# Two FFN layers behind a decayed linear attention: the first two token blocks of layer 1 run in two parts each, with partial sums in SBUF

## The chip, the cores and the metric

The kernel runs on one core of a Trainium2 chip. The metric is the device time of one execution in microseconds (us). Three runs of the kernel before took 987.18, 989.37 and 989.90 us; the median is 989.37 us. A core has the engines PE (matrix multiply, with a separate weight load, PEld), DVE (vector), ACT (scalar), POOL and SP. DMAs are issued from the instruction stream of an engine; here SP issues nearly all of them.

## The reference

```
x = attention(q, k, v, alpha)     # (4, 8, 768, 48); state = alpha_t * state + k_t v_t^T ; y_t = q_t state
x = x.transpose(0, 2, 1, 3).reshape(3072, 384)
h = x @ w_in ; x = max(0.01 * h, h) @ w_out              # layer 1: 384 -> 2048 -> 384
h = x @ moe2_w_in ; x = elu(h) @ moe2_w_out              # layer 2: the same sizes
```

All data are float32, except that the weights come to the chip as pairs of 32-bit words (a float64 each) and are turned there into a high and a low float32r part. Every FFN product is three matmuls: high times high, low times high, high times low.

## The kernel before, in words

**Attention.** The 3072 tokens are 24 units of 128 tokens (`NU`), six to a batch row; a unit holds all 8 heads, as four pairs on partitions 0 to 47 and 64 to 111. `attn_prep` (lines 124 to 138) makes two running products of the decay on DVE (two scans of 1.2 us) and scales k and q. `attn_S` computes the scores of the four pairs and a transpose of k on PE; `attn_S_post` masks them on DVE and, when there is a state from the unit before, makes the decayed state T (lines 166 to 170) in two instructions, one per head of the pair, into a block-diagonal tile with zeros elsewhere. `attn_V` multiplies by v, adds the part of the state (line 186, over all 112 partitions of T) and forms the new state's addend `pu` (line 193). `attn_V_post` writes the result as a high and a low part into the x tiles `xh` and `xl`, and makes the new state S in two instructions (lines 207 to 212).

**Blocks of layer 1.** Four units are one block of 512 tokens; there are six. A unit writes its 384 rows as 3 times 112 partitions and a rest; `gather` (lines 215 to 218) moves the rest into place by six DMAs for `xh` and six for `xl`, on SP's queue. `x` has two buffers, so the units of block j+2 can write only when block j has been read for the last time. A block has 16 steps (m = 0 to 15, a slice of 128 of the 2048 hidden features). Step (j, m) is `ffn1_h` (nine matmuls), `ffn1_g` (an ACT and a DVE instruction, then the split into high and low on ACT and DVE), and `ffn1_y` (nine matmuls into three PSUM banks, which are copied to `x2t` at m = 15, line 288). The h part runs two steps ahead of the y part (`LA`).

**Weights of layer 1.** Slice m of both matrices arrives raw, 768 KB in five DMAs from SP (`stage1`, lines 413 to 421), in one of four tiles `x2t[0..3]`, which later take the results of layer 1. `convert_p` (ACT, lines 232 and 233), `convert_a` (DVE lines 237, 238 and 240, ACT line 241) and `convert_b` (DVE line 244) turn it into the two parts in SBUF; `x2t[4]` and `x2t[5]` are its scratch. When slice m is done, slice m + 4 is loaded. `conv_to` is called in the head (up to 4 slices by the fourth unit) and then ahead of each step of block 0, up to slice s + 5, so that all 16 slices are converted in the steps of block 0.

**Order.** `seq` (lines 615 and 616) is the order of steps: block 0 with all m, block 1 with all m, and so on, then layer 2. The 20 units after the first four are cut in four pieces each (`pieces`), and those of block j + 1 are spread over block j (lines 633 to 637). The order written is a program order: the Tile framework gives every instruction a place on its engine by its own simulated timeline, and may place work of another kind earlier when what it needs is there. Only instructions passed to `pin` keep their program order.

**Loads.** `next_load(u + 3)` after unit u issues the load of `pack` (674 KB) and of `v` (288 KB) on SP. Three buffers each.

**Guard.** In layer 2 the kernel reads all decay data again (`guard_load`, 24 `span` tiles from the pool of `pack`, three buffers) and checks it with two ACT instructions each (`guard_unit`); a slow path `general()` runs only where the check fails. Lines 668 to 676 place one unit every second step from block 1 of layer 2 on. The pool of `pack` also holds half of the output tiles `osb` at each block's end (line 349).

Of the kernel before, what the change touches and what calls it, by code (L numbers as in the profile page):

```python
# [19 lines left out]
def attention_two_layers_kernel(  # L20
# [42 lines left out]
    causal = const.tile([128, C], F32, name="causal")  # L63
    T = const.tile([PR, NP, PD], F32, name="T")
    d0 = const.tile([PR, EXT], F32, name="d0")
# [19 lines left out]
    def constants():  # L85
        make_identity(nc, ident)
        nc.gpsimd.memset(causal, 1.0)
        nc.gpsimd.affine_select(
            out=causal, in_=causal, compare_op=ALU.is_ge, fill=0.0,
            base=0, pattern=[[1, C]], channel_multiplier=-1,  # L90
        )
        nc.gpsimd.memset(T, 0.0)
# [11 lines left out]

    def load_unit(u, first=False):
        t = pack_p.tile([PR, EXT + 2 * NP * C], F32, tag="pack", name="pack")
        if first:
            m = EXT + NP * C
            nc.sync.dma_start(t[:, 0:EXT], seqs[u, :, 0:EXT])
            nc.scalar.dma_start(t[:, EXT:m], seqs[u, :, EXT:m])  # L110
            nc.sync.dma_start(t[:, m:], seqs[u, :, m:])
        else:
            nc.sync.dma_start(t, seqs[u])
        packs[u] = t

    def load_v(u):
        t = v_p.tile([128, NP, 3 * D], F32, tag="v", name="vt")
        nc.sync.dma_start(t.rearrange("s p e -> s (p e)"), vals[u])
        vts[u] = t
# [37 lines left out]
    def attn_S_post(u):  # L157
# [8 lines left out]
        if c > 0:  # L166
            for j in range(2):
                r = slice(64 * j, 64 * j + D)
                nc.vector.tensor_mul(
                    T[r, :, j * D:(j + 1) * D], st["S"][r], d["pe"][r].to_broadcast([D, NP, D]))  # L170

    def attn_V(u):
# [10 lines left out]
        if c > 0:  # L183
            for p in range(NP):
                for j in range(2):
                    nc.tensor.matmul(po[64 * j:64 * j + D, p], lhsT=T[:, p, j * D:(j + 1) * D], rhs=qh[:, p],  # L186
                                     start=False, stop=(p == NP - 1), skip_group_check=True)
        d["po"] = po
        if c < NC - 1:
            pu = ps_a.tile([PR, NP, D], F32, tag="at", name="pu")  # L190
            for p in range(NP):
                for j in range(2):
                    nc.tensor.matmul(pu[64 * j:64 * j + D, p], lhsT=d["kn"][:, p, 64 * j:64 * j + D],
                                     rhs=vt[:, p, 2 * j * D:(2 * j + 1) * D], start=(p == 0), stop=(p == NP - 1),
# [3 lines left out]
    def attn_V_post(u, xh, xl, off):  # L198
# [5 lines left out]
        if c < NC - 1:  # L204
            pu = d["pu"]
            Sn = at_p.tile([PR, NP, D], F32, tag="S", name="S")
            for j in range(2):
                r = slice(64 * j, 64 * j + D)
                if c > 0:
                    nc.vector.tensor_add(Sn[r], pu[r], T[r, :, j * D:(j + 1) * D])  # L210
                else:
                    nc.vector.tensor_copy(Sn[r], pu[r])
# [39 lines left out]
    def ffn1_h(j, m):  # L252
        xh, xl, n = xt[j]
        hp = ps_h.tile([128, n], F32, tag="h", name="hp")
# [19 lines left out]
    ytiles = {}  # L274

    def ffn1_y(j, m):
        n = xt[j][2]
        gh, gl = steps.pop((1, j, m))
        if m == 0:
            ytiles[j] = [ps_y.tile([128, n], F32, tag=f"y{c}", name=f"y{c}") for c in range(KD)]  # L280
        wh, wl = wout[m]
        for c in range(KD):
            for i, (a, x) in enumerate(((wh, gh), (wl, gh), (wh, gl))):
                nc.tensor.matmul(  # L284
                    ytiles[j][c], lhsT=a[:, c * 128:(c + 1) * 128], rhs=x,
                    start=(m == 0 and i == 0), stop=(m == KF - 1 and i == 2),
                )
        if m == KF - 1:
# [8 lines left out]
    def x2_split(j):  # L297
        xh = xs_p.tile([128, KD, 512], F32R, tag="xh", name="xh")
        xl = xs_p.tile([128, KD, 512], F32R, tag="xl", name="xl")
        for c in range(KD):  # L300
# [70 lines left out]
    def xtile(j):  # L371
        if j not in xt:
            n = blocks[j][1] * C
            xt[j] = (
                xs_p.tile([128, KD + 1, 512], F32R, tag="xh", name="xh"),
                xs_p.tile([128, KD + 1, 512], F32R, tag="xl", name="xl"),
                n,
            )
        return xt[j]
# [7 lines left out]
    def attn_post(u, i):  # L387
# [5 lines left out]
        elif i == 2:  # L393
            j = unit_block[u]
            xh, xl, _ = xtile(j)
            attn_V_post(u, xh, xl, (u - blocks[j][0]) * C)
            if u == blocks[j][0] + blocks[j][1] - 1:
                for x in (xh, xl):
                    gather(x, blocks[j][1] * C)
# [57 lines left out]
    class Conversions:  # L457
# [46 lines left out]
    def general():  # L504
# [52 lines left out]
        for j in range(NB):  # L557
            xt.pop(j)
            xh, xl, n = xtile(j)
            for i in range(n // C):  # L560
# [20 lines left out]
    with ExitStack():  # L581
# [25 lines left out]
        for u in range(4):  # L607
# [21 lines left out]
        for s, e in enumerate(seq):  # L629
# [3 lines left out]
            if ph == 1 and pieces:  # L633
                tgt = blocks[j + 1][1] * 4
                done = tgt - len([p for p in pieces if unit_block[p[0]] <= j + 1])
                want = min(tgt, -(-tgt * (m + 1) // (KF - LA)))
# [9 lines left out]
            for p in now:  # L646
                attn_post(*p)
# [18 lines left out]
            if ph == 2 and m == 4 and (j + 1) * 512 < NT:  # L666
                x2_split(j + 1)
            if ph == 2 and j > 0:
                u, odd = divmod(after - 2 * KF, 2)
                if u <= NU and not odd:  # L670
                    if u < NU:
                        guard_load(u)
                    if u > 0:
                        guard_unit(u - 1)
                if u == NU + 1 and not odd:
                    guard()
# [86 lines left out]
```

## Time and profile before

| | us |
|---|---|
| median of three runs | 989.37 |
| the profiled execution | 987.68 |
| its span, first to last instruction | 986.0 |
| PE busy in it | 934.5 (95%) |
| DVE busy | 545.6 (55%) |
| ACT busy | 446.6 (45%) |
| first FFN matmul begins | 59.83 |
| results of block 0 copied out of PSUM from | 190.04 |

The span is the time between the first and the last instruction of the profiled execution; 1.7 us lie around it. Shares of busy time are means over all stages. A matmul's record holds its latency, so that the sum of PE's busy time counts a queue of matmuls as one stretch, and the mean of one record is longer than the distance between two.

### The profile page before, as it was taken

The numbers are of one execution on the slowest core, as the hardware profiler recorded it, in microseconds if no ns is written. First come the engines' busy times: TensorE is split into PE (matmuls) and PEld (weight loads), VectorE is DVE, ScalarE is ACT, GpSimd is POOL, SyncE is SP. The second block draws the span as 40 slices with busy tenths as digits, with TensorE's granted clock in tenths as the row PEclk, the third lists the DMA queues.
The fourth block names the chain that finished last, engine by engine and source line by source line (L and its number), as shares of the span: only waits on it lengthen the run. The fifth ranks groups of instructions, "written<-read, shape, count | busy, mean of one in ns | idle before, by whom it ended". The sixth has DMA issues, their size and how long they took to land.

```text
span 986.0 us, 13236 instructions
## 1 busy us (share of the span) xinstructions
PE 934.5 (95%) x5234; PEld 790.4 (80%) x5234; DVE 545.6 (55%) x916; ACT 446.6 (45%) x783; POOL 1.4 (0%) x9
## 2 busy tenths in 40 slices
PE   4689979899999999999999999999999999999996
PEld 3567757688788788888878889989989989899996
DVE  6799998533657556555559993433433333433332
ACT  1245453332322322233458874574574674444442
POOL 0000000000000000000000000000000000000000
PEclk9779998899999999999999999999999999999999
DMA  9655571000211212211134310030110210000001
GB/s 238 161 173 163 149 184 61 13 1 19 68 51 42 57 41 81 55 44 49 49 96 145 112 49 1 4 105 1 53 55 1 78 30 1 33 1 1 32 1 37
DMA packets 25671, 62.40 MB, mean 63 GB/s; under 512 B 4512, under 2 KB 7584, under 8 KB 25600
## 3 DMA queue, kind: packets, MB, share of 16 engines
q1 hardware_dynamic: 25472, 61.24, 22.0%
q8 instruction: 43, 0.70, 0.3%
q10 hardware_dynamic: 128, 0.23, 0.1%
q14 instruction: 28, 0.23, 0.1%
HBM read 54.37 MB, written 4.72 MB: 60 GB/s over the span
## 4 chain that ended last, share of the span: by engine, by line
PE 80%; DMA 9%; DVE 6%; ACT 2%; SPq 1%; issue 1%; DVEq 0%; ACTq 0%
PE y L284 19%; PE hp L259 18%; PE hp L313 18%; PE o L344 9%; PE oa L344 9%; DMA pack<-in_seqs_dram 3%; DMA x2t<-in_w_dram 3%; PE sc L149 2%; PE po L181 2%; DMA span<-in_seqs_dram 2%; PE po L186 1%; DMA out_dram<-osb 1%; ACT span L496 1%; DVE A L161 1%; DVE x2t L240 1%
## 5 line engine op out<-in xcount | busy, mean ns | idle before, releaser
L82 DVE TENSOR_TENSOR gl<-t,gh 128x512 fp32r<-128x512 f32 x192 | 132.1, 690 | 130.5 <-ACT gh L79 118.9
L79 ACT CAST gh<-t 128x512 fp32r<-128x512 f32 x192 | 118.9, 620 | 170.9 <-PE y L284 60.9
L284 PE MATMUL y<-gh,w 128*128 128x512 f32 x576 | 172.9, 398 | 2.9 <-ACT gh L79 2.9
L259 PE MATMUL hp<-xh,w 128*128 128x512 f32 x576 | 155.1, 402 | 4.6 <-DVE t L268 2.4
L313 PE MATMUL hp<-xh,w 128*128 128x512 f32 x576 | 149.2, 394 | 1.2 <-DVE t L322 1.2
L322 DVE SCALAR_TENSOR_TENSOR t<-t,hp 128x512 f32<-128x512 f32 x96 | 66.0, 687 | 152.2 <-ACT t L321 152.2
L259 PEld LDWEIGHTS hp<-xh,w 128*128 128x128 f32 x576 | 108.8, 192 | 29.6 <-issue 3.2
L284 PEld LDWEIGHTS y<-gh,w 128*128 128x128 f32 x576 | 107.2, 190 | 26.9 <-ACT gh L79 3.7
L313 PEld LDWEIGHTS hp<-xh,w 128*128 128x128 f32 x576 | 106.5, 188 | 19.0 <-DVE t L322 2.2
L284 PE MATMUL y<-gl,w 128*128 128x512 f32 x288 | 105.2, 399 | 0.4 <-DVE gl L82 0.4
L320 ACT ACTIVATE t<-hp 128x512 f32<-128x512 f32 x96 | 57.0, 594 | 105.8 <-PE hp L313 105.7
L268 DVE TENSOR_TENSOR t<-t,hp 128x512 f32<-128x512 f32 x96 | 65.2, 681 | 59.3 <-ACT t L267 59.1
L344 PE MATMUL oa<-w,gh 128*128 128x384 f32 x384 | 96.3, 337 | 1.3 <-ACT gh L79 1.3
L267 ACT ACTIVATE t<-hp 128x512 f32<-128x512 f32 x96 | 56.4, 596 | 90.7 <-PE hp L259 90.5
L344 PE MATMUL o<-w,gh 128*128 128x384 f32 x384 | 95.1, 337 | 1.9 <-ACT gh L79 1.9
L259 PE MATMUL hp<-xl,w 128*128 128x512 f32 x288 | 83.4, 393 | 0.0
L313 PE MATMUL hp<-xl,w 128*128 128x512 f32 x288 | 81.9, 392 | 0.0
L344 PEld LDWEIGHTS o<-w,gh 128*128 128x128 f32 x384 | 70.5, 188 | 7.7 <-ACT gh L79 2.7
L344 PEld LDWEIGHTS oa<-w,gh 128*128 128x128 f32 x384 | 70.1, 188 | 4.5 <-ACT gh L79 1.7
L284 PEld LDWEIGHTS y<-gl,w 128*128 128x128 f32 x288 | 53.6, 189 | 13.6 <-DVE gl L82 1.3
L313 PEld LDWEIGHTS hp<-xl,w 128*128 128x128 f32 x288 | 54.1, 188 | 12.2
L259 PEld LDWEIGHTS hp<-xl,w 128*128 128x128 f32 x288 | 54.3, 189 | 11.7 <-issue 0.2
(94 smaller groups left out, 1005.6 us busy)
## 6 DMA issues: line engine op xcount, KB each, us to landing
pack<-in_seqs_dram SPq DMA_DIRECT2D x23, 674.2 KB, 5.6
stg<-in_w_dram SPq DMA_DIRECT2D x28, 384.0 KB, 3.1
x2t<-in_w_dram SPq DMA_DIRECT2D x20, 384.0 KB, 4.6
vt<-in_vals_dram SPq DMA_DIRECT2D x24, 288.0 KB, 5.1
span<-in_seqs_dram SPq DMA_DIRECT2D x24, 226.2 KB, 2.7
x2t<-in_w_dram SPq DMA_DIRECT2D x32, 144.0 KB, 4.5
out_dram<-osb SPq DMA_DIRECT2D x24, 192.0 KB, 2.2
x2t<-in_w_dram SPq DMA_DIRECT2D x32, 48.0 KB, 4.3
```

Source lines behind the costliest of these rows:

```text
L79: nc.scalar.copy(dst, src)
L82: (lo_engine or nc.vector).tensor_sub(lo, src, dst.bitcast(F32))
L149: nc.tensor.matmul(sc[j][:, p], lhsT=kS[r, p, :], rhs=qh[r, p, :], start=True, stop=True)
L181: nc.tensor.matmul(po[64 * j:64 * j + wide, p], lhsT=vt[:, p, 2 * j * D:2 * j * D + wide], rhs=A[:, j, p], start=(p == 0), stop=(p == NP - ...
L259: nc.tensor.matmul(hp, lhsT=a[:, kk, :], rhs=x[:, kk, :n], start=(i == 0), stop=(i == 3 * KD - 1))
L267: nc.scalar.activation(t, hp, ACTF.Copy, scale=0.01)
L268: nc.vector.tensor_max(t, t, hp)
L284: nc.tensor.matmul(ytiles[j][c], lhsT=a[:, c * 128:(c + 1) * 128], rhs=x, start=(m == 0 and i == 0), stop=(m == KF - 1 and i == 2),)
L313: nc.tensor.matmul(hp, lhsT=a[:, kk, :], rhs=x[:, kk, :], start=(i == 0), stop=(i == 3 * KD - 1))
L320: nc.scalar.activation(t, hp, ACTF.Relu, scale=-1.0)
L322: nc.vector.scalar_tensor_tensor(out=t, in0=t, scalar=-1.0, in1=hp, op0=ALU.add, op1=ALU.max)
L344: nc.tensor.matmul(otiles[j][i], lhsT=a[:, i * 128:(i + 1) * 128], rhs=x, start=(m == 0 and n == 0), stop=(m == KF - 1 and n == 2),)
```

## The change

It has six parts.

1. `seq` begins with steps 0 to 3 of block 0, steps 0 to 3 of block 1, steps 4 to 15 of block 0, steps 4 to 15 of block 1. After the first part of a block its three PSUM sums are copied to `x2t` (ACT); after the second, DVE adds the PSUM sums to what lies there. So `x2t[0]` and `x2t[1]` are no longer free for raw weights after slices 0 and 1: slices 4 to 15 use `x2t[2]` and `x2t[3]` in turn, and slice m + 2 is loaded when slice m is done.
2. The conversion is spread over more steps: two slices in the head, two in steps 0 and 1, then three for every four steps up to step 17. Units 4 to 7 are placed in steps 0 and 1, units 8 to 11 from step 6 to step 29.
3. T and S are one DVE instruction each over all 112 partitions; T is no longer block-diagonal, and the matmuls with it use 48 partitions per head.
4. The loads of `pack` and `v` from unit 3 on are issued by ACT.
5. `xh` and `xl` are halves of one tile, and `gather` moves both by six DMAs.
6. The guard's units stand at m = 6, 8, 10, 12 and 14 of every block of layer 2, from block 0 on.

```diff
-            for j in range(2):
-                r = slice(64 * j, 64 * j + D)
-                nc.vector.tensor_mul(
-                    T[r, :, j * D:(j + 1) * D], st["S"][r], d["pe"][r].to_broadcast([D, NP, D]))
+            T = at_p.tile([PR, NP, D], F32, tag="cT", name="T")
+            nc.vector.tensor_mul(T, st["S"], d["pe"].to_broadcast([PR, NP, D]))
...
-                    nc.tensor.matmul(po[64 * j:64 * j + D, p], lhsT=T[:, p, j * D:(j + 1) * D], rhs=qh[:, p],
+                    r = slice(64 * j, 64 * j + D)
+                    nc.tensor.matmul(po[r, p], lhsT=d["T"][r, p], rhs=qh[r, p],
...
-            nc.sync.dma_start(x[hi:hi + 16, b // 2, :n].bitcast(F32), x[lo:lo + 16, KD, :n].bitcast(F32))
+            nc.sync.dma_start(x[hi:hi + 16, :, b // 2, :n].bitcast(F32), x[lo:lo + 16, :, KD, :n].bitcast(F32))
...
+    FIRST = 4
+    def parts(j, m):
+        return m == 0 or (j < 2 and m == FIRST), m == KF - 1 or (j < 2 and m == FIRST - 1)
...
-                if c == 1:
+                if j < 2 and m == KF - 1:
+                    nc.vector.tensor_add(dst[:, c], ytiles[j][c], dst[:, c])
+                elif c == 1 and j > 1:
...
-            load_unit(u)
-            load_v(u)
+            load_unit(u, eng=nc.scalar)
+            load_v(u, eng=nc.scalar)
...
-        t = x2t[m % 4].rearrange("p c f -> p (c f)").bitcast(I32)
+        t = x2t[m if m < 4 else 2 + m % 2].rearrange("p c f -> p (c f)").bitcast(I32)
...
-                if self.layer == 1 and m + 4 < KF:
-                    stage1(m + 4)
+                if self.layer == 1 and m >= 2 and m + 2 < KF:
+                    stage1(m + 2)
...
-            conv_to(PC[u] // 2)
-        seq = [(1, j, m) for j in range(NB) for m in range(KF)]
+            conv_to(min(PC[u] // 2, LA))
+        head, tail = range(FIRST), range(FIRST, KF)
+        seq = [(1, j, m) for ms in (head, tail) for j in range(2) for m in ms]
+        seq += [(1, j, m) for j in range(2, NB) for m in range(KF)]
...
+                if s < 2 * KF:
+                    want = 8 * s + 8 if s < 2 else 16 + max(0, -(-16 * (s - 5) // (2 * KF - LA - 6)))
+                    done = 4 * (NU - 4) - len(pieces)
...
-            converting = ph == 1 and j == 0
+            converting = s < 2 * KF
-                conv_to(s + PS // 2)
+                conv_to(s + 3 if s < 2 else FIRST + 3 * (s - 1) // 4)
...
-            if ph == 2 and j > 0:
-                u, odd = divmod(after - 2 * KF, 2)
+            if ph == 2 and m >= KF - 10 and m % 2 == 0:
+                u = 5 * j + (m - KF + 10) // 2
```

## Rows read from the trace of the kernel before

**Rows 1.** The page: part 1, busy time of each engine, and from part 2 the granted clock of PE in 40 slices of 24.65 us.

```profile
PE 934.5 (95%) x5234; PEld 790.4 (80%) x5234; DVE 545.6 (55%) x916; ACT 446.6 (45%) x783; POOL 1.4 (0%) x9
...
PEclk9779998899999999999999999999999999999999
```

**Rows 2.** Busy time by stretch: the stretch and its length, then busy us and instruction count of each engine, granted clock, DMA share and GB/s.

```profile
0.00:59.80 59.80, 34.74 (x276) 29.83 (x276) 45.79 (x82) 15.10 (x21) 1.45 (x9) 0.84 0.74 194
59.80:166.20 106.40, 96.89 (x645) 73.02 (x645) 100.77 (x161) 50.45 (x74) 0.00 (x0) 0.94 0.52 142
...
190.50:261.00 70.50, 70.50 (x333) 57.02 (x332) 26.33 (x39) 20.68 (x36) 0.00 (x0) 1.00 0.08 20
...
575.00:978.00 403.00, 398.45 (x1996) 359.38 (x1994) 152.02 (x236) 218.60 (x390) 0.00 (x0) 1.00 0.08 24
```

**Rows 3.** The chain that ended last, in order of time: start, us, what. The first is one y part of a step in block 1; the other two are the same piece of work in blocks 3 and 4.

```profile
214.43 2.04 PE y L284 x9
...
337.32 2.95 PE hp L259 x12
...
419.35 2.95 PE hp L259 x12
```

**Rows 4.** PE's groups of FFN matmuls between 59.8 and 261 us: count, busy us, mean ns of a record, idle before.

```profile
L259 PE MATMUL hp<-xh,w 128*128 128x512 f32 x204 | 59.4, 421 | 3.2 <-DMA xh<-xh 2.1 <-DVE t L268 1.0
L284 PE MATMUL y<-gh,w 128*128 128x512 f32 x192 | 56.9, 402 | 2.9 <-ACT gh L79 2.9
L284 PE MATMUL y<-gl,w 128*128 128x512 f32 x96 | 34.4, 408 | 0.4 <-DVE gl L82 0.4
L259 PE MATMUL hp<-xl,w 128*128 128x512 f32 x102 | 30.2, 400 | 0.0
```

**Rows 5.** The timeline around the first FFN matmul: start, us, engine, line, what, count, in brackets the idle time before and what ended it.

```profile
53.11 0.58 ACT L202 CAST xh<-po 112x512 fp32r<-112x512 f32 x1 [2.01 <-PE po L186]
...
53.80 4.61 SPq L218 DMA_DIRECT2D xh<-xh  x6
...
55.29 0.68 DVE L203 TENSOR_TENSOR xl<-po,xh 112x512 fp32r<-112x512 f32 x1
...
58.45 3.75 SPq L218 DMA_DIRECT2D xl<-xl  x6
```

**Rows 6.** DVE's groups between 59.8 and 166.2 us: count, busy us, mean ns, idle before.

```profile
L244 DVE TENSOR_TENSOR w<-x2t,w 128x768 fp32r<-128x768 f32 x14 | 13.2, 949 | 0.9 <-ACT w L241 0.9
L240 DVE CUSTOM_DVE_ANT_0 x2t<-x2t,x2t 128x1536 uint16<-128x1536 uint16 x14 | 13.1, 947 | 0.0
L238 DVE SCALAR_TENSOR_TENSOR x2t<-x2t 128x768 int32<-128x768 int32 x13 | 12.3, 949 | 0.0
L268 DVE TENSOR_TENSOR t<-t,hp 128x512 f32<-128x512 f32 x14 | 9.5, 681 | 1.6 <-ACT t L267 1.5
...
L161 DVE TENSOR_TENSOR A<-sc,causal 128x512 f32<-128x512 f32 x13 | 8.8, 680 | 0.0
L130 DVE TENSOR_TENSOR_SCAN E<-pack,d 112x517 f32<-112x517 f32 x7 | 8.6, 1225 | 1.6 <-DMA pack<-in_seqs_dram 1.6
...
L237 DVE TENSOR_SCALAR x2t<-x2t 128x768 int32<-128x768 int32 x13 | 7.1, 551 | 0.1
...
L169 DVE TENSOR_TENSOR T<-S,pe 48x192 f32<-48x192 f32 x10 | 3.4, 344 | 0.2
L210 DVE TENSOR_TENSOR S<-pu,T 48x192 f32<-48x192 f32 x8 | 2.8, 346 | 1.0 <-PE pu L193 0.8
```

**Rows 7.** DVE's waits in the first 60 us: line, what it waited for, us in total, times, longest.

```profile
DVE E L130 <- DMA pack<-in_seqs_dram: 11.1, 5, 4.7
```

**Rows 8.** The timeline of unit 3's load: ACT's copy that follows the last read of unit 0's pack, SP's issues, and DVE's scan of unit 3.

```profile
18.03 0.58 ACT L202 CAST xh<-po 112x512 fp32r<-112x512 f32 x1
...
22.79 0.34 SPq L113 DMA_DIRECT2D pack<-in_seqs_dram  x1
...
30.46 1.24 DVE L130 TENSOR_TENSOR_SCAN E<-pack,d 112x517 f32<-112x517 f32 x1 [4.74 <-DMA pack<-in_seqs_dram]
```

**Rows 9.** The timeline of slice 15 of the weights: first issue of its load, the two ACT instructions on it, and DVE's last reading of the raw tile (of slices 14 and 15 together).

```profile
141.93 0.31 SPq L418 DMA_DIRECT2D x2t<-in_w_dram  x1
...
147.38 0.91 ACT L233 ACTIVATE x2t<-x2t 128x768 int32<-128x768 uint16 x1
...
158.63 0.92 ACT L232 ACTIVATE x2t<-x2t 128x768 f32<-128x768 f32 x1
...
162.96 1.82 DVE L240 CUSTOM_DVE_ANT_0 x2t<-x2t,x2t 128x1536 uint16<-128x1536 uint16 x2
```

**Rows 10.** Layer 2: the first and the last of the five places where PE stood idle for 0.4 us or more between 580 and 978 us, and the guard's two instructions on ACT (min, median and max ns, first and last start).

```profile
657.03 0.98 PE L344 MATMUL oa<-w,gh 128*128 128x384 f32 x4 [1.28 <-ACT gh L79]
...
795.17 1.33 PE L344 MATMUL o<-w,gh 128*128 128x384 f32 x6 [1.01 <-ACT gh L79]
...
L495 ACT ACTIVATE span<-span,bias x24: 708/722/727, 643.4 to 796.3; 112x512 f32<-112x512 f32 x24
L496 ACT ACTIVATE span<-span,bias x24: 705/710/730, 644.5 to 797.9; 112x512 f32<-112x512 f32 x24
```

**Rows 11.** The timeline of a unit's second half in block 1, behind an h part of the FFN: the first weight loads (PEld), and the product with T on PE.

```profile
242.92 0.49 PEld L181 LDWEIGHTS po<-A,vt 128*48 128x48 f32 x9 [0.35 <-issue]
...
243.53 1.13 PE L186 MATMUL po<-pack,T 112*48 112x128 f32 x15
```

More of the change, by code (lines that the diff above doesn't have):

```diff
@@ L103, in attention_two_layers_kernel, with load_unit @@
     st = {}
-    def load_unit(u, first=False):
+    def load_unit(u, first=False, eng=None):
         t = pack_p.tile([PR, EXT + 2 * NP * C], F32, tag="pack", name="pack")
@@ L112, in load_unit, with load_v @@
         else:
-            nc.sync.dma_start(t, seqs[u])
+            (eng or nc.sync).dma_start(t, seqs[u])
         packs[u] = t
-    def load_v(u):
+    def load_v(u, eng=None):
         t = v_p.tile([128, NP, 3 * D], F32, tag="v", name="vt")
-        nc.sync.dma_start(t.rearrange("s p e -> s (p e)"), vals[u])
+        (eng or nc.sync).dma_start(t.rearrange("s p e -> s (p e)"), vals[u])
         vts[u] = t
@@ L192, in attn_V @@
                 for j in range(2):
-                    nc.tensor.matmul(pu[64 * j:64 * j + D, p], lhsT=d["kn"][:, p, 64 * j:64 * j + D],
+                    r = slice(64 * j, 64 * j + (D if j else 64))
+                    nc.tensor.matmul(pu[r, p], lhsT=d["kn"][:, p, r],
                                      rhs=vt[:, p, 2 * j * D:(2 * j + 1) * D], start=(p == 0), stop=(p == NP - 1),
@@ L206, in attn_V_post @@
             Sn = at_p.tile([PR, NP, D], F32, tag="S", name="S")
[L207 to L212, printed above, removed]
+            if c > 0:
+                nc.vector.tensor_add(Sn, pu, d["T"])
+            else:
+                nc.vector.tensor_copy(Sn, pu)
             st["S"] = Sn
@@ L278, in ffn1_y @@
         gh, gl = steps.pop((1, j, m))
-        if m == 0:
+        first, last = parts(j, m)
+        if first:
             ytiles[j] = [ps_y.tile([128, n], F32, tag=f"y{c}", name=f"y{c}") for c in range(KD)]
@@ L285, in ffn1_y @@
                     ytiles[j][c], lhsT=a[:, c * 128:(c + 1) * 128], rhs=x,
-                    start=(m == 0 and i == 0), stop=(m == KF - 1 and i == 2),
+                    start=(first and i == 0), stop=(last and i == 2),
                 )
-        if m == KF - 1:
+        if last:
             t0 = blocks[j][0] * C
@@ L297, in x2_split @@
     def x2_split(j):
-        xh = xs_p.tile([128, KD, 512], F32R, tag="xh", name="xh")
-        xl = xs_p.tile([128, KD, 512], F32R, tag="xl", name="xl")
+        t = xs_p.tile([128, 2, KD + 1, 512], F32R, tag="x", name="x")
+        xh, xl = t[:, 0], t[:, 1]
         for c in range(KD):
@@ L373, in xtile @@
             n = blocks[j][1] * C
[L374 to L378, printed above, removed]
+            t = xs_p.tile([128, 2, KD + 1, 512], F32R, tag="x", name="x")
+            xt[j] = t[:, 0], t[:, 1], n, t
         return xt[j]
@@ L394, in attn_post @@
             j = unit_block[u]
-            xh, xl, _ = xtile(j)
+            xh, xl, _, t = xtile(j)
             attn_V_post(u, xh, xl, (u - blocks[j][0]) * C)
             if u == blocks[j][0] + blocks[j][1] - 1:
-                for x in (xh, xl):
-                    gather(x, blocks[j][1] * C)
+                gather(t, blocks[j][1] * C)
             next_load(u + 3)
@@ L558, in general @@
             xt.pop(j)
[L559 removed]
+            xh, xl, n, _ = xtile(j)
             for i in range(n // C):
@@ L633, in attention_two_layers_kernel @@
             if ph == 1 and pieces:
-                tgt = blocks[j + 1][1] * 4
-                done = tgt - len([p for p in pieces if unit_block[p[0]] <= j + 1])
-                want = min(tgt, -(-tgt * (m + 1) // (KF - LA)))
+                if s < 2 * KF:
+                    want = 8 * s + 8 if s < 2 else 16 + max(0, -(-16 * (s - 5) // (2 * KF - LA - 6)))
+                    done = 4 * (NU - 4) - len(pieces)
+                else:
+                    tgt = blocks[j + 1][1] * 4
+                    done = tgt - len([p for p in pieces if unit_block[p[0]] <= j + 1])
+                    want = min(tgt, -(-tgt * (m + 1) // (KF - LA)))
                 now, pieces = pieces[:max(0, want - done)], pieces[max(0, want - done):]
-            converting = ph == 1 and j == 0
+            converting = s < 2 * KF
             if converting:
-                conv_to(s + PS // 2)
+                conv_to(s + 3 if s < 2 else FIRST + 3 * (s - 1) // 4)
             if n:
@@ L645, in attention_two_layers_kernel @@
                 attn_pe(*p)
-            for p in now:
                 attn_post(*p)
@@ L667, in attention_two_layers_kernel @@
                 x2_split(j + 1)
-            if ph == 2 and j > 0:
-                u, odd = divmod(after - 2 * KF, 2)
[L670 to L675, printed above, removed]
+            if ph == 2 and m >= KF - 10 and m % 2 == 0:
+                u = 5 * j + (m - KF + 10) // 2
+                if u < NU:
+                    guard_load(u)
+                if 0 < u <= NU:
+                    guard_unit(u - 1)
+                if u == NU:
                     guard()
```

5 lines of the change are left out of this document (2 added, 3 removed).

## Prediction

> **What bounds the kernel now.** I read the page's busy shares first: PE 95%, the others at 55% or less [rows 1], so the end is set by PE, and time can come only from PE's idle or slow stretches or from its amount of work. Then busy time by stretch [rows 2], where three kinds of stretch show. From 190.5 to 261 us and in nearly all of layer 2 PE is full. Up to 59.8 us there is no FFN matmul at all, and DVE has 45.8 of the 59.8 us. From 59.8 to 166.2 us DVE is the full engine (100.8 of 106.4), while PE's record still says 96.9; that record is misleading, since its records hold latency. A count shows it. In steady state nine matmuls take 2.04 us [rows 3], 0.227 each. Between 59.8 and 261 us PE ran 204 + 192 + 96 + 102 = 594 of them [rows 4], worth 134.7 us. A unit of attention costs PE 4.2 us: equal work of two following blocks begins 82.0 us apart, 16 steps of 4.08 are 65.3, and the rest of 16.7 belongs to four units [rows 3]. Units 4 to 11, eight, are 33.4. So 168 us of work stood in 201.2 us, and 33 us were lost there, all before 190 us. The granted clock is part of the same loss: it shows below full only in slices of the first 200 us [rows 1]. In layer 2, 403.0 - 398.45 = 4.55 us of PE are idle [rows 2], in five gaps between 657 and 796 us, at the time of the guard's instructions on ACT [rows 10].
>
> I therefore follow three sums: the end of block 1 (261 us now), the gaps in layer 2, and the amount of PE work. Everything between 261 us and layer 2 is PE-bound and keeps its length unless PE's work changes.
>
> **Order of steps and spread of the conversion.** A slice costs DVE 0.551 + 0.949 + 0.947 + 0.949 = 3.40 us, a step 2 x 0.681 = 1.36 (line 268, and the split's subtraction of the same shape) [rows 6]. By 166.2 us DVE has done all 16 slices, 14 steps and the attention that the order lets run ahead: 45.8 + 100.8 = 146.6 us busy and 19.6 idle [rows 2]. After the change PE has 19 or 20 steps' h parts to run by the time the last slice is needed (step 17) in place of 14, so the same weights feed more PE work. DVE's bill up to the last slice becomes: 146.6; plus 5 steps x 1.36 = 6.8; minus the halves of T and S that fall away, 9 + 9 instructions of 0.345 (10 and 8 of them stand in [rows 6], the others and the S of batch starts in the head) = 6.2; together 147. Its idle time is now mostly the head's wait for pack data, 11.1 us [rows 7]. Of that, 4.7 us is unit 3's data: its load was issued at 22.79 us, 4 us after its buffer was free, behind weight loads on SP, and DVE stood from 25.7 to 30.46 us [rows 8]. Issued by ACT right behind the copy at 18.03 it can land before DVE asks. So idle goes to about 15, and DVE alone would finish the slices at 147 + 15 = 162 us.
>
> The second limit is the raw tiles, two in place of four from slice 4 on. A tile's round is: issue to ACT's first instruction 147.38 - 141.93 = 5.45 us; that instruction 0.91; from the second instruction at 158.63 to the end of DVE's reading at 164.78, 6.15 [rows 9]. That is 12.5 us without the wait in the middle, 6.3 per slice with two tiles. Slices 4 to 15 start when units 4 to 7, which now stand in steps 0 and 1, let DVE go: first matmul at about 55 us, then 36 us of DVE work, so at 91. These are four units, less the preparation of one that is done before, 23.5; two slices, 6.8; and four steps, 5.5. A unit is two scans of 1.23, five instructions of full width at 0.68 to 0.69 like the mask, T and S at 0.35 each and 0.34 for two small ones, 6.9 in all, of which 4.2 are preparation [rows 6]. Then 91 + 12 x 6.3 = 167. The two limits agree, and I take 168 us for the last slice. Ends: 150, if attention of block 2 no longer runs ahead of it, and 228, if the round stays at the 22.9 us of [rows 9], 11.4 per slice.
>
> After that PE has y parts 17 to 31 and as many h parts, 30 x 2.04 = 61.2 us [rows 3], and what is left of units 8 to 11, between 0 and 16.7; I take 9, half. Block 1 ends at 168 + 70 = 238 us instead of 261: -23. PE's own floor is 55 + 168 = 223, so 15 of the 33 us stay lost, mostly in steps 0 and 1, where DVE needs 36 us and PE has 25 to do.
>
> Costs at nothing: the six extra copies out of PSUM on ACT and the six adds on DVE fall where DVE has 26.3 of 70.5 us and ACT 20.7 [rows 2]; uncovered they would be six times about 0.7 us. PE waits for a PSUM bank at two more block switches, but an h part of 2.04 us stands between two y parts and covers a copy.
>
> **Loads on ACT.** Two issues per unit, 0.3 to 0.4 us each as on SP [rows 8], 21 units: some 16 us of ACT, which has 55% free [rows 1]. The wait that moves along is for the last reader of the buffer: for pack PE's product with T, which ACT's copy ahead of it awaits anyway, and for v the product after it, about 1 us as for the product with T [rows 11]. Queued behind it on ACT are the FFN's ACT instructions, and PE waits for those after two steps, 8 us; so nothing, and 21 us if each wait of 1 us reached PE. SP keeps weights and gathers, and nothing waits behind a unit's load on it any more.
> By the Trainium skill (DMA: Bandwidth & Descriptors, "Issuing engines are not separate DMA queues") DMAs from two issuers share the same 16 engines, and a second issuer saves only issue time. By that rule unit 3's data would come hardly earlier, the idle time would stay near 19.6, and the sum would be about 4 us higher; what runs here show is only that SP's issues were late, not how two issuers share.
>
> **Gather.** The first FFN matmul needs only `xh`, whose six DMAs began at 53.80 while `xl` was written at 55.97 [rows 5]. The joint six start after the latter and take about 3.75 us to issue as those of `xl` did: 2 us later for the first matmul, and 2.5 earlier for the last byte. In the middle of a block's steps it hides behind PE. DVE's chain ahead of it is shorter by one slice (3.4) and the six half instructions of T and S (2.1) and the 4.7 above, of which I count 7 in all: first matmul at 59.8 - 7 + 2 = 55. This is inside the -23.
>
> **T on 48 partitions.** The product with T, 16 records at about 0.07 us [rows 11], now sits in two disjoint quarters of the array, so it may take half, -0.5 us; but its shape differs from the product before and after it, and at a change of shape the weight load stood idle for 0.35 us ("issue") [rows 11], twice +0.7 at the most. Net +0.2, between -0.5 and +0.7; ten units with a state lie in the PE-bound blocks: +2, from -5 to +7.
> The Trainium skill (TensorEngine Tiling (Array Packing), "Key Properties") says that changing the tiling mode, not just the tile, drains TensorE, which speaks against this part; with the drain and no gain from two tiles the sum would be 5 us higher than mine. The 0.35 us agree with a drain, and no row shows two tiles at once in this shape.
>
> **Guard.** The 24 units ran between 643 and 798 us in three bursts, one after each block end; eight are 8 x (0.72 + 0.71) = 11.4 us of ACT [rows 10]. Five in a burst are 7.2. A step needs (218.6 - 24 x 1.43) / 96 = 1.9 us of ACT in 4.2 [rows 2], so the delay drops from more than the two steps of lookahead to about one, and the gaps go: -4.4, bounds 0 and -4.55.
>
> **Sum.** 987.7 - 23 - 4.4 + 2 = 962.3 against the profiled execution, whose 986.0 us of span have 1.7 around them; that execution lies 1.7 below the median, so 964 as a median.
>
> **Rivals.**
> A. The raw tiles bind somewhat more: 7.8 us per slice, last slice at 185, block 1's end at 255, total 979 + 1.7 = 981. For: the 5.45 us of [rows 9] are one load, and units' loads now run beside it from a second queue. Against: DVE takes a slice in 3.4 us when free.
> B. Slower: the same two tiles, when a slice sits unread as slice 15 did (11 us between ACT's two instructions [rows 9]). The gains outside are 4.4 - 2 = 2.4 us, so it turns at a last slice at 193 us, 8.5 us per slice; at 9.5 the end is at 205 + 70 = 275, total 1001. For: 22.9 us of round in [rows 9]. Against: that wait is one of four tiles standing in line for a full DVE; with two there is less line.
> C. PE comes near its floor: last slice at 152, end at 225, and PE work -2: 947.
> D. The simulated timeline places the attention and the slices as before, so that the new order does nothing: 0 in the blocks, total 987; against it speaks that h and y parts of block 1 do not need later slices.
>
> **Chances.** Forecast 0.55 (its own range 955 to 974), A 0.2, B 0.09, C 0.12, D 0.04. Less than 0.3%, 3 us, is not told from no change. Faster 0.86, same 0.05, slower 0.09. The range for 8 in 10 is 946 to 985.
>
> **What would show it.** Right: first FFN matmul at 53 to 57 us; DVE line 244 for slice 15 ending near 168; the first layer's block 1 leaving PSUM near 238; block period then 82 us; no gap over 0.4 us in layer 2; the wait of unit 3's scan gone. Wrong: ACT waiting for weight DMAs over 60 us in total, DVE less than 85% busy between 90 and 168 us (then the tiles bind), or PE idle in blocks 2 to 5 behind an ACT issue.

## The result: 1% slower, and the profile after

Measured side by side, the changed kernel took 998.20 us (median of 4) and the kernel before 988.58 us (median of 4). The ratio is 1.010, with a 95% interval from 1.0078 to 1.0122, so it is slower by 1% where 2.6% faster was forecast. The profiled execution took 1000.04 us, with a span of 998.2.

The page of the changed kernel answers to [rows 1]: PE is busy 9 us longer. Its granted clock (PEclk, in tenths of full speed, 40 slices of 24.95 us) is lower than before in the second to the fourth slice and in the ninth.

```profile
PE 943.3 (94%) x5234; PEld 792.8 (79%) x5234; DVE 533.2 (53%) x880; ACT 446.7 (45%) x785; POOL 1.1 (0%) x8
...
PEclk9567999889999999999999999999999999999999
```

Busy time by stretch, with the columns of [rows 2]. The stretches end where the first FFN step begins, just before slice 4's conversion, at the last slice's, and where block 1 leaves PSUM. The last one lies in layer 2; the 5.8 us in which PE is idle there come after its last matmul, which ends at 991.2 us.

```profile
0.00:59.80 59.80, 33.91 (x277) 27.41 (x277) 41.80 (x72) 12.91 (x18) 1.08 (x8) 0.68 0.67 175
59.80:120.00 60.20, 54.84 (x400) 41.09 (x401) 44.52 (x75) 17.86 (x29) 0.00 (x0) 0.87 0.43 116
120.00:211.50 91.50, 76.25 (x348) 57.28 (x347) 66.44 (x96) 44.27 (x65) 0.00 (x0) 0.91 0.37 107
211.50:285.00 73.50, 72.10 (x364) 57.15 (x364) 35.27 (x57) 22.12 (x38) 0.00 (x0) 0.98 0.15 41
...
595.50:997.00 401.50, 395.72 (x1990) 358.65 (x1989) 152.26 (x237) 218.10 (x390) 0.00 (x0) 1.00 0.09 27
```

The column to look at is the third of busy times, DVE. Before, DVE was nearly full from 59.8 to 166.2 us (100.8 of 106.4, [rows 2]). Now it is busy for 44.5 of 60.2 us and then for 66.4 of 91.5, about 73%, and yet the last slice is done 44 us later (211.4 against 167.1). Between 120 and 211.5 us neither PE (76.3 of 91.5) nor DVE nor the DMA engines (0.37) are full: much of this time goes in waits of one engine for another. Some links of these chains stand in the timeline around 105 us:

```profile
104.66 0.67 DVE L202 TENSOR_TENSOR x<-po,x 112x512 fp32r<-112x512 f32 x1
105.36 4.82 SPq L215 DMA_DIRECT2D x<-x  x6
...
112.92 3.51 PE L256 MATMUL hp<-x,w 128*128 128x512 f32 x14
...
119.94 0.67 DVE L265 TENSOR_TENSOR t<-t,hp 128x512 f32<-128x512 f32 x1
...
121.71 0.56 DVE L234 TENSOR_SCALAR x2t<-x2t 128x768 int32<-128x768 int32 x1
```

Units 4 to 7 end at 105 us, the gather follows, then the h parts of block 1's first two steps, then their g (line 265), and only then DVE touches slice 4 (line 234). The chain that ended last runs in these 17 us through one more link, the load of the next `pack`, for which DVE stood still ahead of the first of these g (117.98):

```profile
110.69 5.32 DMA pack<-in_seqs_dram
116.03 1.25 DVE E L128
...
119.94 0.67 DVE t L265
...
121.71 0.56 DVE x2t L234
```

It is the data of unit 11, since the planner has placed the preparation of units 9 to 11 ahead of slice 4. SP's queue shows when the slices' loads were issued, and what came after them:

```profile
77.77 0.32 SPq L419 DMA_DIRECT2D x2t<-in_w_dram  x1
...
85.38 0.31 SPq L419 DMA_DIRECT2D x2t<-in_w_dram  x1
...
105.36 4.82 SPq L215 DMA_DIRECT2D x<-x  x6
127.21 0.32 SPq L419 DMA_DIRECT2D x2t<-in_w_dram  x1
```

The load of slice 4 was issued at 77.77 us and that of slice 5 at 85.38; ACT first read them at 87.41 and 98.62, DVE at 121.71 and 123.39. SP issued no weights for 40 us, until slice 4's raw tile was free. The last slice, counterpart of [rows 9], in the timeline:

```profile
196.88 0.31 SPq L419 DMA_DIRECT2D x2t<-in_w_dram  x1
...
202.04 0.90 ACT L230 ACTIVATE x2t<-x2t 128x768 int32<-128x768 uint16 x1 [4.36 <-DMA x2t<-in_w_dram]
...
210.48 0.96 DVE L241 TENSOR_TENSOR w<-x2t,w 128x768 fp32r<-128x768 f32 x1 [0.90 <-ACT w L238]
```

It ends at 211.4 us. Block 1 leaves PSUM with the additions of line 296, the last of them after 283.8 us, against 260.8 us for the last copy before. The chains to 121.71 us stood in no part of the prediction.

### The profile page after: what moved, and what is told of

Read it like the earlier page. It is cut to its first block, busy times and chain, and to the rows that moved or that the text cites. A ratio compares the mean times of both kernels' runs of the same rounds, so it can differ in the third digit from the quotient of the medians.

```text
span 998.2 us, 13124 instructions
## 1 busy us (share of the span) xinstructions
PE 943.3 (94%) x5234; PEld 792.8 (79%) x5234; DVE 533.2 (53%) x880; ACT 446.7 (45%) x785; POOL 1.1 (0%) x8
## 4 chain that ended last, share of the span: by engine, by line
PE 86%; DMA 7%; DVE 4%; ACT 1%; issue 1%; SPq 1%; ACTq 0%; DVEq 0%
PE hp L318 20%; PE y L287 19%; PE hp L256 19%; PE oa L349 10%; PE o L349 10%; DMA pack<-in_seqs_dram 4%; DMA x2t<-in_w_dram 3%; PE sc L147 2%; PE po L178 2%; PE po L184 2%; PE pu L192 1%; DVE x2t L237 1%; PE pk L152 1%; DVE E L128 1%; DVE x2t L235 1%
## 5 line engine op out<-in xcount | busy, mean ns | idle before, releaser
L256 PE MATMUL hp<-x,w 128*128 128x512 f32 x864 | 223.0, 403 | 12.9 <-DVE w L241 4.1
L318 PE MATMUL hp<-x,w 128*128 128x512 f32 x864 | 215.4, 393 | 0.0
L256 PEld LDWEIGHTS hp<-x,w 128*128 128x128 f32 x864 | 165.2, 193 | 51.4 <-issue 8.4
L318 PEld LDWEIGHTS hp<-x,w 128*128 128x128 f32 x864 | 160.7, 188 | 29.3
L287 PE MATMUL y<-gh,w 128*128 128x512 f32 x576 | 177.2, 407 | 6.7 <-ACT gh L78 6.7
L349 PE MATMUL oa<-w,gl 128*128 128x384 f32 x192 | 63.0, 337 | 0.0
L326 ACT ACTIVATE t<-t 128x512 f32<-128x512 f32 x96 | 60.8, 633 | 2.3
L349 PE MATMUL o<-w,gl 128*128 128x384 f32 x192 | 61.0, 336 | 0.0
L147 PEld LDWEIGHTS sc<-pack 48*128 48x128 f32 x384 | 34.4, 213 | 20.2 <-issue 9.7
```

Source lines behind the costliest of these rows:

```text
L147: nc.tensor.matmul(sc[j][:, p], lhsT=kS[r, p, :], rhs=qh[r, p, :], start=True, stop=True)
L256: nc.tensor.matmul(hp, lhsT=a[:, kk, :], rhs=x[:, kk, :n], start=(i == 0), stop=(i == 3 * KD - 1))
L287: nc.tensor.matmul(ytiles[j][c], lhsT=a[:, c * 128:(c + 1) * 128], rhs=x, start=(first and i == 0), stop=(last and i == 2),)
L318: nc.tensor.matmul(hp, lhsT=a[:, kk, :], rhs=x[:, kk, :], start=(i == 0), stop=(i == 3 * KD - 1))
L326: nc.scalar.activation(t, t, ACTF.Exp, scale=-1.0)
L349: nc.tensor.matmul(otiles[j][i], lhsT=a[:, i * 128:(i + 1) * 128], rhs=x, start=(m == 0 and n == 0), stop=(m == KF - 1 and n == 2),)
```

## The experiments

The changed kernel is called "the changed order" here; "the old order" has parts 1 and 2 undone. "Layer 2" is the span less the start of layer 1's last recorded copy out of PSUM; where the trace shows two copies as one row, that row's start is taken, so these two columns can be off by up to 1 us against each other.

| kernel | ratio to before (95%) | median us | block 1's last copy or addition | last copy of layer 1 | layer 2 |
|---|---|---|---|---|---|
| before | 1 | 988.58 | 260.8 | 574.9 | 411.1 |
| changed | 1.010 (1.0078 to 1.0122) | 998.20 | 283.8 | 594.2 | 404.0 |
| e1 old order, parts 3 to 6 | 0.9774 (0.9739 to 0.9810) | 970.19 | 247.4 | 565.8 | 405.6 |
| e2 changed, four raw tiles | 1.0010 (0.9991 to 1.0029) | 992.57 | 275.4 | 585.5 | 406.1 |
| e3 changed, slices two ahead | 0.9859 (0.9824 to 0.9894) | 977.72 | 255.6 | 568.3 | 403.9 |
| e4 both of these | 0.9910 (0.9875 to 0.9945) | 983.39 | 267.7 | 579.3 | 405.3 |
| e5 changed, conversion free | 0.9985 (0.9967 to 1.0003) | 990.59 | 272.3 | 584.3 | 403.4 |
| e6 e1 without part 4 | 0.9712 (0.9685 to 0.9740) | 963.93 | 246.8 | 560.2 | 404.3 |
| e7 e1 without parts 3 and 6 | 0.9811 (0.9783 to 0.9839) | 972.68 | 250.4 | 561.5 | 406.1 |
| e8 e4, gather on ACT | 0.9917 (0.9889 to 0.9944) | 983.41 | 261.4 | 575.4 | 404.0 |
| e9 before + part 5 | 0.9807 (0.9773 to 0.9840) | 971.12 | 253.7 | 564.7 | 404.6 |
| e10 before + part 6 | 0.9947 (0.9930 to 0.9964) | 985.37 | 265.7 | 580.8 | 405.6 |
| e11 e3 without part 4 | 0.9868 (0.9827 to 0.9909) | 976.45 | 257.7 | 568.6 | 403.7 |
| e12 e6, two slices in the head | 0.9881 (0.9842 to 0.9921) | 979.67 | 261.8 | 576.0 | 403.9 |
| e13 before + one x tile, 12 DMAs | 0.9935 (0.9915 to 0.9954) | 982.62 | 259.9 | 575.4 | 405.4 |
| e14 e6, slices two further ahead | 0.9815 (0.9780 to 0.9850) | 970.18 | 249.7 | 564.9 | 403.3 |

The kernel before, run beside each group, had medians from 989.7 to 991.8 us in the groups of e1 to e14, so columns of single profiles and medians differ by a few us from one line to another; the ratios decide.

### Undoing the order, the ring, the lateness

e1 undoes parts 1 and 2:

```diff
-        seq = [(1, j, m) for ms in (head, tail) for j in range(2) for m in ms]
-        seq += [(1, j, m) for j in range(2, NB) for m in range(KF)]
+        seq = [(1, j, m) for j in range(NB) for m in range(KF)]
...
-                conv_to(s + 3 if s < 2 else FIRST + 3 * (s - 1) // 4)
+                conv_to(s + PS // 2)
```

The change has one more edit, which its list of six parts does not name: in the loop over the steps, a piece's work on DVE and ACT is now written right behind the same piece's work on PE, and no longer behind that of all pieces of the step. e1 undoes it too, so here it counts with parts 1 and 2; e2 to e5, e8 and e11 keep it, and no run separates it.

> Parts 1 and 2 undone (old step order, old spread of units and slices, four raw tiles, no partial sums), parts 3 to 6 kept. Theory (start and ring: the loss of the changed kernel comes from slices that start 30 us late behind units 4 to 7, and from two raw tiles after that): 978 to 984 us, that is 989 less 7 in layer 2, plus 1 to 2 for T, with block 1 leaving PSUM near 260 us. Rival 1 (loads on ACT, the joint gather or T are at fault): 993 or more, block 1 leaving PSUM later than 270. Rival 2 (the order itself, that is the chain of units 4 to 7 ahead of block 1's first step, and not the tiles): 978 to 984 too; it is told from the theory by the next three.

970.19 us, better than either theory said. Parts 1 and 2 therefore cost 3.3% (1.010 against 0.9774), and parts 3 to 6 together gain 2.3%.

e2 gives the changed order four raw tiles; the two more lie where the weights of slices 14 and 15 come later:

```diff
+        if m >= 4 and m % 4 < 2:
+            t = more[m % 4]
+        else:
+            t = x2t[m % 4].rearrange("p c f -> p (c f)").bitcast(I32)
```

> The changed kernel with four raw tiles again (the two more stand in the memory of the last two slices' weights until those are converted), order and spread as changed. Theory (start and ring): the late start stays (slice 4's first DVE instruction still near 121 us), but then a slice takes 5 to 6 us instead of 7.6, last slice at 185 to 192 instead of 211, and 975 to 982 us. Rival 2 (the order alone, tiles do not matter): within 3 us of 998. Rival 3 (the ring alone): 975 or less, last slice before 180.

992.57 us, a miss: slice 4 still began at 123.3 us, and the last slice ended at 204.5, so twelve slices took 6.8 us each instead of (211.4 - 121.7)/12 = 7.5. The ring of two tiles costs about 8 us (block 1 leaves PSUM at 275.4 instead of 283.8) and not the rest.

e3 keeps two tiles and only writes the conversion two slices further ahead, so that slice 4 stands before units 4 to 7 and slice 5 before units 6 and 7:

```diff
-                conv_to(s + 3 if s < 2 else FIRST + 3 * (s - 1) // 4)
+                conv_to(s + 5 if s < 2 else FIRST + 2 + 3 * (s - 1) // 4)
```

> The changed kernel with two raw tiles, but slices 4 and 5 are converted ahead of units 4 to 7's last pieces (conversion runs two slices ahead of the changed kernel's through all steps). Theory (start and ring): the start comes 15 to 20 us earlier, the round of two tiles stays at 7 to 7.6 us per slice, last slice at 190 to 200, 983 to 992 us. Rival 2 (the order alone): within 3 us of 998, since units 4 to 7 then only come later. Rival 3 (the ring alone): within 3 us of 998.

977.72 us: one line gives 20 us, more than was expected of it. From e3's timeline of DVE, the first instructions of slices 4 and 6 and the last slice's last:

```profile
87.40 0.55 DVE L234 TENSOR_SCALAR x2t<-x2t 128x768 int32<-128x768 int32 x1
...
121.61 0.55 DVE L234 TENSOR_SCALAR x2t<-x2t 128x768 int32<-128x768 int32 x1
...
182.06 0.96 DVE L241 TENSOR_TENSOR w<-x2t,w 128x768 fp32r<-128x768 f32 x1 [0.90 <-ACT w L238]
```

Slice 4 starts 34 us earlier and the last slice ends 28 us earlier. The chain itself is still there: slice 6 begins at 121.61 us, where slice 4 began in the changed kernel. But two slices now stand ahead of it, and the ten from slice 6 on take (183.0 - 121.6)/10 = 6.1 us each, with two tiles. In its table by stretch PE has no idle time from 120 to 300 us, at full clock, and most of what is left is in 60 to 120 us:

```profile
60.00:120.00 60.00, 51.53 (x390) 39.52 (x390) 44.49 (x73) 22.17 (x35) 0.00 (x0) 0.88 0.51 142
120.00:180.00 60.00, 60.00 (x301) 46.44 (x300) 55.35 (x82) 36.68 (x56) 0.00 (x0) 1.00 0.43 123
```

> Both edits together: four raw tiles and slices two ahead. Theory (start and ring): last slice at 165 to 175 us, block 1 leaving PSUM near 240 to 250, 958 to 970 us. Rival 2 (the order alone): 990 or more. Rival 3 (the ring alone): same as with four tiles alone.

e4 joins both edits and was expected to be the best; at 983.39 us it is worse than e3 alone. Its gather was issued at 114.96 us, behind the loads of slices 8 and 9 on SP, though its data was written by 107.8, and block 1's first step began at 118.97 instead of 108.42. e8 tried that explanation by issuing the gather from ACT:

> Four raw tiles and slices two ahead, with the gather issued by ACT instead of SP. Theory (the gather of units 4 to 7 stood on SP behind the loads of slices 8 and 9, issued at 114.96 though its data was written by 107.8): block 1's first step at 112 us instead of 119, and 972 to 979 us instead of 983. Rival (four tiles' loads take the DMA engines, whoever issues): within 3 us of 983.

Block 1's first step came at 110.17, but the median is 983.41, as before: the explanation is not borne out. Why four tiles cost 6 us beside an early conversion stays open; a larger wait for the units' data goes with it (DVE's waits for pack up to 130 us: e3, then e4, then e8).

```profile
DVE E L128 <- DMA pack<-in_seqs_dram: 13.4, 8, 3.4
```
```profile
DVE E L129 <- DMA pack<-in_seqs_dram: 14.9, 9, 3.4
```
```profile
DVE E L129 <- DMA pack<-in_seqs_dram: 17.8, 11, 3.5
```

e5 takes away the written order of the conversion altogether (`pinned[0] = False`):

> The changed kernel, with the conversions' program order no longer kept: the framework's simulated timeline may place each slice as early as its data allows. Theory (the written order makes slices wait: 'late start'): slice 4 starts by 95 us, and the time falls to 975 to 988 us, like the run with slices two ahead. Theory (the ring of two tiles is what paces): slices start earlier but still take over 7 us each, 990 or more. It may also go wrong in a third way: slices placed ahead of units delay the chain to block 1's first step, 998 or more.

By its numbers the second of these came true: slice 4 starts at 43.91 us, a slice takes (135.75 - 43.91)/12 = 7.7 us, and the time is 990.59 us. But the ring is not what ends block 1, and the mechanism of the third shows. From its timeline of DVE, the last unit of block 1 and the last slice; and of PE, block 1's first step:

```profile
123.43 0.68 DVE L202 TENSOR_TENSOR x<-po,x 112x512 fp32r<-112x512 f32 x1
...
134.79 0.96 DVE L241 TENSOR_TENSOR w<-x2t,w 128x768 fp32r<-128x768 f32 x1 [0.51 <-ACT w L238]
```
```profile
129.60 1.62 PE L256 MATMUL hp<-x,w 128*128 128x512 f32 x3 [1.56 <-DMA x<-x]
```

All slices are done by 136 us, 32 us before my 168, and yet the time falls by little. Now the first FFN matmul is late (66.94 us instead of 59.73) and so is the chain to block 1's first step (129.6), since slices stand ahead of units on DVE, and the steps 4 to 15 of block 0 are written behind it. I read this so: the changed order has two chains that compete for DVE, and the one that stands second sets the end. In no variant did the new order itself pay: at its best it took 976.45 us (e11) and 977.72 (e3), the old order with the same other parts 963.93 (e6) and 970.19 (e1).

### Parts 3 to 6, one at a time

> The old order with parts 3, 5 and 6, but the loads of units back on SP (part 4 undone). The old order with all four parts took 970 us, 12 us less in layer 1 than the kernel before. If the loads on ACT gave that: 976 to 984 us, unit 3's scan waiting 4 us or more again and slices' loads issued later. If they gave nothing (two issuers share the same DMA engines): 969 to 973 us.

e6 puts the loads back on SP (`load_unit(u)` for `load_unit(u, eng=nc.scalar)`). It gained 6 us, which lies below both ranges: the loads on ACT had cost time instead of giving it. Unit 3's stall did come back, but the next unit began no later for it. DVE's scans of units 3 and 4, first in e1 (loads on ACT), then in e6 (on SP):

```profile
26.20 1.24 DVE L128 TENSOR_TENSOR_SCAN E<-pack,d 112x517 f32<-112x517 f32 x1 [0.70 <-DMA pack<-in_seqs_dram]
38.29 1.22 DVE L128 TENSOR_TENSOR_SCAN E<-pack,d 112x517 f32<-112x517 f32 x1
```
```profile
32.02 1.24 DVE L128 TENSOR_TENSOR_SCAN E<-pack,d 112x517 f32<-112x517 f32 x1 [4.66 <-DMA pack<-in_seqs_dram]
38.38 1.23 DVE L128 TENSOR_TENSOR_SCAN E<-pack,d 112x517 f32<-112x517 f32 x1
```

And DVE's waits for pack up to 260 us are nearly the same in total, again e1 and then e6:

```profile
DVE E L128 <- DMA pack<-in_seqs_dram: 17.5, 11, 3.1
```
```profile
DVE E L128 <- DMA pack<-in_seqs_dram: 18.8, 10, 4.7
```

The Trainium skill (DMA: Bandwidth & Descriptors, "Issuing engines are not separate DMA queues") says that a second issuer saves only issue time; the two totals agree. It does not say where the 6 us come from. In e1's profile block 4's last copy on ACT follows block 3's by 86.3 us (412.98 to 499.27), against 81.9 in e6 (412.46 to 494.40), 4.4 us of the difference; there PE waits for a late gather, and its granted clock is 0.70 from 490 to 495 us, against 1.00 in the 10 us before:

```profile
490.91 6.28 PE L256 MATMUL hp<-x,w 128*128 128x512 f32 x18 [1.79 <-DMA x<-x]
```

Whether this comes with every execution of e1 is not shown. In the changed order the same edit, e11, gave nothing that can be told:

> The changed order with two raw tiles and slices two ahead, loads of units back on SP (part 4 undone). In the old order the loads on ACT cost 6 us. If that holds in the new order too: 969 to 974 us instead of 977.7. If SP's queue then holds the units' loads behind weights and gathers in steps 0 and 1: 980 or more, with block 1's first step later than 108 us.

976.45 against 977.72 us.

> The old order with parts 4 and 5, but T and S in two operations each (part 3 undone) and the guard where it was (part 6 undone). The two show in different stretches. Part 6: layer 2 takes 410 us again instead of 403 to 405, with five gaps on PE. Part 3: the period of blocks 2 to 5 is 82.0 us instead of 82.4, and in blocks 0 and 1 the halves cost DVE 6 us, so that block 1 leaves PSUM at 250 to 255 us instead of 248. Total 975 to 983 us. If part 3 gave the 12 us of layer 1, block 1 ends at 258 or later.

e7 undoes parts 3 and 6 in the old order: 972.68 us, 2.5 more than e1 and below what was expected. Layer 2 (406.1 us) is hardly longer than in the others although the guard stands where it did before, and PE has no gap of 0.4 us there. Block 3's copies are 81.9 us behind block 2's (332.91 to 414.82) against 82.4 in e1 (330.54 to 412.98): part 3 costs some 0.1 us per unit in steady state.

e9 then adds part 5 alone to the kernel before:

> The kernel before with part 5 alone (x as one tile, six joint DMAs). The two old-order runs without part 4 and without parts 3 and 6 both ended layer 1 at 561 to 562 us, 13 to 14 earlier than the kernel before, and share only part 5. If part 5 gave that: 974 to 980 us, block 1 leaving PSUM at 245 to 252. If each of parts 3 and 4 gives it as well, or the framework's placement does by chance: 985 to 991 us. My forecast's price for part 5 was a gain of about 0 to 3 us.

971.12 us, below the lower of the two ranges: the six joint DMAs and the single tile, which I had priced at next to nothing, give 1.9%. e13 splits it: `xh` and `xl` halves of one tile, but moved by twelve DMAs. Against e9 (`gather` itself is the old one again):

```diff
-                gather(t, blocks[j][1] * C)
+                for i in range(2):
+                    gather(t[:, i], blocks[j][1] * C)
```

> The kernel before with xh and xl as halves of one tile, as in part 5, but still moved by twelve DMAs in the old way. If the six DMAs fewer on SP give the gain of part 5: 988 to 992 us, no change. If the one tile gives it, through the places that the framework's planner then chooses for instructions: 969 to 975 us.

982.62 us, between the two. Layer 1 ends as before (575.4), and layer 2 is 5.7 us shorter; the six DMAs fewer are then worth 1.3%, nearly all of it in layer 1 (575.4 to 564.7). The sizes, from the tables of DMA issues (count, KB, median us to landing), of the kernel before and of e9:

```profile
xh<-xh SPq DMA_DIRECT2D x36, 32.0 KB, 4.3
xl<-xl SPq DMA_DIRECT2D x36, 32.0 KB, 2.0
```
```profile
x<-x SPq DMA_DIRECT2D x36, 64.0 KB, 4.3
```

The Trainium skill (DMA: Bandwidth & Descriptors, "Rules for kernel authors") tells one to join many small transfers, since below 64 KB one pays mostly overhead. The result agrees. What shows is SP's queue, where twelve DMAs took from 118.31 to 126.4 us and six in one go take 4 to 5. But by which path it reaches the end is not shown. It is not the slices: the last one ends at 169.3 us in e9 and at 167.1 in the kernel before. Between 120 and 210 us the two, the kernel before first, differ in how many matmuls they run and in the granted clock, while DVE does about the same.

```profile
120.00:210.00 90.00, 80.26 (x420) 62.06 (x416) 65.05 (x103) 35.62 (x56) 0.00 (x0) 0.92 0.28 77
```
```profile
120.00:210.00 90.00, 81.98 (x469) 64.34 (x469) 67.61 (x108) 35.82 (x57) 0.00 (x0) 0.98 0.26 75
```

> The kernel before with part 6 alone. Forecast of the prediction: 4.4 us faster, 985 to 988 us beside 991.7, layer 2 at 406 us or less instead of 410.5 and no gap. Rival (the old-order run with the old guard had no gaps either and took 405 in layer 2, so the guard's place is not the cause): the same as before, with gaps in layer 2 that depend on how layer 1 ends.

Part 6 alone: 0.5% faster, 985.37 against 991.17 us, and layer 2 at 405.6; the size was right, with one gap of 0.87 us left. But the single tile removes the same loss (e13: 405.4), and both together hardly more (403.3 to 406.1 in the kernels that have both): it looks like one loss with two ways out.

### How far ahead is enough

e12 and e14 move the conversion in the best kernel, e6. e12 does two slices in the head instead of four (`conv_to(min(PC[u] // 2, LA))`, then `conv_to(min(s + PS // 2, 3 + 2 * s))`), e14 writes `conv_to(s + 7)` for `conv_to(s + 5)`.

> The best so far (old order, parts 3, 5 and 6, loads on SP: 963.9 us, first FFN matmul at 63.6) with two slices in the head instead of four, the next ones two per step until the old lead is reached. If the head's DVE time sets the first matmul: first matmul at 56 to 58 us and 958 to 962 us. If DVE's bill up to the last slice sets block 1's end: 963 to 967 us with an earlier first matmul and PE waiting for weights between 60 and 120 us.

> The best so far (old order, parts 3, 5 and 6, loads on SP, 963.9 us) with the slices converted two steps further ahead (up to slice s + 7 ahead of step s instead of s + 5). Two slices later cost this order 16 us and two slices earlier gave the changed order 20 us. If lateness still costs here: 958 to 962 us. If the lead is already enough and DVE's total bill decides: 963 to 967, or slower, since slices then push the steps' own DVE work back.

979.67 and 970.18 us against 963.93. Later costs 16 us, more than either theory said, even with a first FFN matmul at 60.10 us instead of 63.59; further ahead costs 6. The table by stretch of e6, whose lead was the best of the three, has hardly any idle time on PE from 60 us on, with DVE full until 120.

```profile
60.00:120.00 60.00, 59.42 (x331) 43.72 (x332) 58.30 (x90) 35.45 (x53) 0.00 (x0) 0.93 0.67 178
120.00:180.00 60.00, 60.00 (x384) 45.49 (x383) 50.77 (x80) 24.73 (x42) 0.00 (x0) 1.00 0.32 86
```

e6 (old order, parts 3, 5 and 6) is the fastest kernel measured: 2.9% under the kernel before (0.9685 to 0.9740).

## Why the prediction was wrong, step by step

**The step that failed is the start in "91 + 12 x 6.3 = 167".** The 91 us were 55 for the first FFN matmul and DVE's bill behind it: 36 us of work, as if DVE did only this and without a wait. DVE began slice 4 at 121.7 us: 31 of the 44 us by which the last slice came late. The first matmul came 4.7 us late. From there to slice 4 went 62.0 us in place of 36: DVE was busy for 46.3 of them, with the preparation of units 6 to 11 where the sum counted three units, and idle for 15.7. Its instructions are links of a chain through PE, ACT, SP, the gather and the loads of `pack`, and the program order kept slice 4 behind the g of block 1's first step: units 4 to 7 left DVE at 105.3 us, and slice 4 began 16 us later. e3, which only writes the slices two further ahead, got 28 us back at the last slice.

**The round of 6.3 us per slice** was 7.5: 12 x 1.2 = 14 us more. e2 with four tiles has 6.8 and its last slice ends 7 us earlier; but in e3 two tiles are enough for 6.1. So the working of the round was not far off for the tiles alone, and what it left out were waits: between 121.7 and 211.4 us DVE waited 7.2 us for `pack`, 6.6 for ACT ahead of a g and 5.1 for raw weights. Rival B had the slower side by "a slice sits unread", with its turn at a last slice at 193 us; the last slice came at 211. Its mechanism was half the story: DVE left slices 4 and 5 unread for 34 and 25 us after ACT's first reading, but not because two tiles are few. With four tiles they sat as well: in e2 slice 4's load was issued at 78.16 us and DVE began it at 123.26.

**"After that 70 us" held.** From the last slice to block 1's last addition it was 283.8 - 211.4 = 72 us. In e2 it was 71 and in e3 73. It holds only where the slices come last: in e5 it was 137.

**DVE's two limits.** That DVE and the raw tiles would agree at 162 and 167 us was no confirmation. Both counted throughput, and neither held the latency of the new order. DVE was to be under 85% busy between 90 and 168 us only if the tiles bound; it was 63.3 of 78 us busy (81%), but e2 shows that the tiles were the smaller part. ACT's waits for weight DMAs came to 46.5 us up to 215 us, under the 60 of the other sign.

**First FFN matmul** at 55 us: it came at 59.7, as before. Unit 3's wait did go (its scan began at 25.50 instead of 30.46 us, with 0.28 us of wait), but that gain ended with the next units: DVE's wait for `pack` in the first 60 us was 11.0 us in all, against 11.1 before [rows 7], so the idle time that the sum took away was still there. e1 and e6 show the same.

**Gather.** "2 us later for the first matmul, and 2.5 earlier for the last byte" was the largest single error among the parts: alone it gives 20 us. In the sum it was invisible, because parts 1 and 2 lost more.

**Guard and layer 2.** -4.4 us was forecast; layer 2 is 7.1 us shorter (411.1 to 404.0), and between 600 and 960 us PE is idle for 0.0 us instead of 4.4. e10 confirms the size for the kernel before; with part 5 in place the guard's part is no longer needed.

**T on 48 partitions.** The period of blocks 2 to 5 rose by 0.4 us, 0.1 per unit, where 0.2 was forecast. Right, and small.

**Loads on ACT** at nothing: 6 us in the old order (e1 against e6), nothing to be told in the changed order (e3 against e11).

## What to carry to other kernels

When work is reordered, count the longest chain of waits through all engines from the new order, not only each engine's bill; a busy share that falls while the end comes later points to such a chain. Where conversions are held in program order, the place at which each is written is a lever of its own: two slices earlier gained 20 us (e3) and two later cost 16 (e12), though two further ahead than needed cost 6 (e14), while the reordering that they served gained nothing in any variant. Measure the parts of a change singly: one of six parts gained 20 us, two lost some 30, and the sum showed neither.

## What was not expected of the hardware and the planner

Six DMAs of 64 KB in place of twelve of 32 KB were worth 1.3% of the whole time, with only six gathers in the kernel. Merging two tiles into one, with the same DMAs, shortened layer 2 by 5.7 us, a stage that has no gather. I take it that the framework's planner places the instructions differently when tiles or DMAs change; no run shows it by itself. Such shifts of about 5 us are as large as several of the parts that were priced here.
